# Float64 weight words turned into float32 with a leaky rectifier, and a new planned order, in an attention and gated-MLP kernel

## The chip, the cores and the metric

The kernel runs on one core of one Trainium2 chip. The metric is the device time of one execution in microseconds. A core has a matrix engine (TensorE, PE in the profile), three engines for elementwise work (VectorE or DVE, ScalarE or ACT, GpSimd or POOL), and SyncE (SP), which here issues all transfers between the main memory and the on-chip memory SBUF. TensorE writes its sums to the memory PSUM.

## The reference

There are 8 batches of 576 positions. In each, 8 heads of width 64 compute masked softmax attention; heads 0 to 3 see the last 32 positions, heads 4 to 7 see earlier positions that are congruent modulo 32. The heads' outputs, side by side, are the input x (576 by 512) of a gated MLP:

```
scores = where(mask, (q @ k.T) / 8, -1e9);  attn = exp(scores - max) / (sum + 1e-9)
x      = attn @ v                               # all heads, (B, 576, 512)
h      = maximum(x @ w_in, 0);  u, v = halves of h, 512 columns each
v_n    = (v - mean(v)) / sqrt(var(v) + 1e-6)    # over the 512 columns
v_s    = w_spatial @ v_n + b_spatial[:, None]   # over the positions
out    = (u * v_s) @ w_out
```

q, k, v and w_spatial come as float32. w_in (512 by 1024) and w_out (512 by 512) come as float64. The diff is about how these two reach the chip's arithmetic.

## The kernel before

**Work and tiles.** Two heads make an attention tile t; four tiles make a batch, the first two of them local (heads 0 to 3), the other two strided. A tile is loaded as q, k and v, its scores are formed on TensorE (`s`), masked, exponentiated and normalised on the three elementwise engines, turned by a VectorE transpose (`pc`), copied piece by piece into the layout of the next matmul (`ptl` for local tiles, `pts` for strided), multiplied by v on TensorE (`po`), and written as x.

**Three products for one.** Each float32 operand of the large products is split into a high part, rounded to TensorE's format (`rnd`, a one-input copy), and a low part, the rest (`rest`, a two-input subtraction, L372). Every product is then three matmuls: high by high, high by low, low by high. This holds for x, w_in, w_spatial, the normalised v (`vn`), the gated values (`g`) and w_out.

**Stages of a batch.** `moe_1` forms the v half of h (L800), its statistics (L767 to L780), the normalisation (L787) and the split, and the u half (L842). `moe_tail` does the last 64 positions. `moe_2` applies w_spatial (L922, L934, L935), multiplies by u (L944) and projects (L964). The two weights must be on the chip in split form before a batch's products with them can run, and w_spatial with its tail rows `wtail` before `moe_2`.

**Float64 weights.** `weight` loads a 128 by 512 piece of w_in or w_out (a "half" of w_in is such a piece of its u or its v columns) as pairs of 32-bit words and turns it into float32 in place. There are twelve pieces. Read as a float32, the top word has the sign, eight of the eleven exponent bits, and then three exponent bits and twenty mantissa bits where a float32 has its mantissa. The steps are: multiply the top word, as a float32, by 2**-112, which moves the exponent to float32's bias (L674 on ScalarE or L676 on VectorE); shift the low word right by 29 (L681); shift the top word left by 3 and merge it with the low bits (L688), which pushes the sign out; merge the sign back in (L696). `rnd` and `rest` then split the result into `w_in_sb` or `w_out_sb`.

**Staging space.** The first four pieces use the later space of `vn`; the following pieces alternate between the two buffers each of `u` and `g`. The raw spatial weights and wtail use buffers of the x ring, which has eight. q, k and v have two buffers each, so a load of a third tile waits until the first one's is used.

**Order.** Nothing is written in order by hand. Every step is added to a `Program` with a key (its due time), the engines that could do it and a cost on each. `order` then plays the program forward: each engine takes the ready step with the lowest key, and a step that several engines could do goes to the one that ends it first. KEYS holds the due times: `a` of the first eight attention tiles, `v` and `u` of the pieces of w_in by block of rows, `o` those of w_out, `s` and `t` of w_spatial and wtail, `fill` and `cst` of the setup. A weight's load is due 25 before its key, a tile's q, k and v 34, 33 and 20 before. Later steps have due times by their place in the plan of batches. `near` is how far ahead in keys TensorE looks for another attention matmul once it is in that mode. Before the time `dpt` (in thousands of ns) the planner adds the charge `dp` to VectorE's end time wherever it compares VectorE with another engine for a step:

```python
            held = KEYS["dp"][0] if now < KEYS["dpt"][0] * 1000.0 else 0.0
            other = [
                (begin(n, o, max(free[o] + queue(o, n), ready_at[n][o])) + c + held * (o == DVE), o)
                for o, c in ops[n][1]
                if o != e
            ]
            if other and min(other)[0] < now + cost + held * (e == DVE):
                e = min(other)[1]
```

A step's `port` names engines on which the planner holds it back while the other of VectorE and GpSimd runs a step that has itself such a mark. `rnd` steps have the mark (DVE,), `rest` steps that may run on GpSimd (DVE, POOL); the normalisation of the scores (L416) and the subtraction of the row maximum (L570) also have (DVE, POOL). Before WARM_END, `fillers` adds matmuls on zeros (L1085) into TensorE's long planned gaps.

Of the kernel before, what the change touches and what calls it, by code (L numbers as in the profile page):

```python
# [12 lines left out]
AF = mybir.ActivationFunctionType  # L13
ALU = mybir.AluOpType
# [22 lines left out]
TAIL = S - 4 * P  # L37
NT = 4
KEYS = {
    "a": (-2171.5, -625.6, -893.2, -356.9, 1325.6, -222.2, -52.3, 22.3,),  # L40
    "v": (-407.2, -245.7, -878.2, -1404.4,),
    "u": (-86.3, -477.1, 14.3, -106.1,),
    "s": (434.1, 1240.4, 3115.7, 449.8,),
    "o": (212.8, 23.8, 371.3, 2176.0,),
    "t": (1572.7,),
    "lead": (0.24,),
    "dp": (2136,),
    "dpt": (102.36,),
    "fill": (-432.8, 2205.8, 217.3, 421.5, 2743.1, 2393.8,),
    "cst": (-952.3,),  # L50
    "near": (280.07,),
}
WARM_END, WARM_GAP, WARM_COST, WARM_COLS, WARM_SHARE = 110000.0, 800.0, 427.0, 256, 0.5
FETCHED, FETCH_COST = 200.0, 32.0
# [5 lines left out]
PE, ACT, DVE, POOL, DMA = "tensor", "scalar", "vector", "gpsimd", "sync"  # L60
# [67 lines left out]
class Program:  # L128
# [37 lines left out]
    def order(self):  # L166
# [37 lines left out]
        while len(issued) < len(ops):  # L204
            best = None
            for e in ENGINES:
                while wait[e] and taken[wait[e][0][1]]:
                    heapq.heappop(wait[e])
                while ready[e] and taken[ready[e][0][1]]:
                    heapq.heappop(ready[e])  # L210
                if ready[e]:
                    at = free[e]
                elif wait[e]:
                    at = max(free[e], wait[e][0][0])
                else:
                    continue
                if best is None or at < best[0]:
                    best = (at, e)
            now, e = best
            while wait[e] and wait[e][0][0] <= now:  # L220
                n = heapq.heappop(wait[e])[1]
                if not taken[n]:
                    heapq.heappush(ready[e], (ops[n][0], n))
            n = heapq.heappop(ready[e])[1]
            if e == PE:
                stock = min(FETCHED, stock + (now - since) / FETCH_COST)
                since = now
                other = []
                if n in self.tiled:
                    if self.tiled[n] > stock:  # L230
                        other = [op for op in ready[PE] if op[1] not in self.tiled]
                elif mode:
                    other = [
                        op for op in ready[PE]
                        if self.tiled.get(op[1], FETCHED) < stock
                        and op[0] < ops[n][0] + KEYS["near"][0]
                    ]
                if other:
                    heapq.heappush(ready[PE], (ops[n][0], n))
                    ready[PE].remove(min(other))  # L240
                    heapq.heapify(ready[PE])
                    n = min(other)[1]
            cost = dict(ops[n][1])[e]
            if e == PE:
                cost += 45.0 * ((n in self.tiled) != mode)
                mode = n in self.tiled
                stock -= self.tiled.get(n, 3)
                cost += FETCH_COST * max(0.0, -stock)
            now = begin(n, e, max(free[e], ready_at[n][e]))
            held = KEYS["dp"][0] if now < KEYS["dpt"][0] * 1000.0 else 0.0  # L250
            other = [
                (begin(n, o, max(free[o] + queue(o, n), ready_at[n][o])) + c + held * (o == DVE), o)
                for o, c in ops[n][1]
# [4 lines that stand above are left out]
                cost = dict(ops[n][1])[e]  # L258
                now = begin(n, e, max(free[e], ready_at[n][e]))
            taken[n] = True  # L260
            if e in self.port.get(n, ()):
                held_by[e] = (now, now + cost)
            free[e] = now + cost
            issued.append((now, n, e))
            for m in after[n]:
                for o in ENGINES:
                    lag = LAT[e][o]
                    ready_at[m][o] = max(ready_at[m][o], now + cost + lag)
                left[m] -= 1
                if not left[m]:  # L270
                    release(m)
# [34 lines left out]
def attention_moe(ctx, tc, qT, kT, vl, vs, cst, w_in, w_out, wsp, wtail, out):  # L306
# [6 lines left out]
    add = prog.add  # L313
# [341 lines left out]
    def weight(key, src, n, dst, tok, stage):  # L655

        buf, i = stage
        if src.dtype == F32:  # L660
            val = lambda: buf().bitcast(F32).rearrange(FLAT[len(buf.ring.shape)])[:, 2 * i * n : 2 * i * n + n]
            load(key - 25, val, src, [(buf, i, 0), (buf, i, 1)], P * n * 4)
        else:
            raw = lambda dt: buf().bitcast(dt).rearrange(FLAT[len(buf.ring.shape)])[
                :, 2 * i * n : 2 * (i + 1) * n
            ]
            half = lambda j, dt=I32: raw(dt).rearrange("p (n t) -> p n t", t=2)[:, :, j]
            low, top = (buf, i, 0), (buf, i, 1)
            val = lambda dt=F32: half(1, dt)
            load(key - 25, lambda: raw(I32), src.bitcast(I32), [low, top], P * n * 8)  # L670

            def scale(eng):
                if hasattr(eng, "activation"):
                    eng.activation(val(), val(), AF.Copy, scale=2.0**-112)  # L674
                else:
                    eng.tensor_scalar(val(), val(), 2.0**-112, None, op0=ALU.mult)  # L676

            add(key, [(ACT, 95 + 0.833 * n), (DVE, 70 + 0.52 * n)], scale, [], [top], port=(DVE, POOL))
            add(
                key, [(DVE, 70 + 0.52 * n)],  # L680
                lambda eng: eng.tensor_scalar(  # L681
                    half(0), half(0), 29, None, op0=ALU.logical_shift_right
                ),
                [], [low], port=(DVE, POOL),
            )
            add(
                key, [(DVE, 70 + 1.04 * n)],
                lambda eng: eng.scalar_tensor_tensor(  # L688
                    half(0), half(1), 3, half(0),
                    op0=ALU.logical_shift_left, op1=ALU.bitwise_or,  # L690
                ),
                [top], [low], port=(DVE, POOL),
            )
            add(
                key, [(DVE, 70 + 1.04 * n)],
                lambda eng: eng.scalar_tensor_tensor(  # L696
                    half(1), half(1), -0x80000000, half(0),
                    op0=ALU.bitwise_and, op1=ALU.bitwise_or,
                ),
                [low], [top], port=(DVE, POOL),  # L700
            )
        lo_in = [(buf, i, 0), (buf, i, 1)] if src.dtype == F32 else [top]
        rnd(key, n, lambda: dst(0), val, lo_in, [(*tok, 0)])
# [290 lines left out]
    lead = min(nb, 2)  # L994
# [168 lines left out]
```

## Time and profile before

| | |
|---|---|
| median of 3 runs | 540.17 us (539.29 to 542.32) |
| profiled execution | 543.93 us, its span 542.1 us |
| mean granted TensorE clock | 0.984 of full speed |
| PE busy | 515.1 us (95%), 6500 matmuls |
| DVE busy | 323.9 us (60%) |
| ACT busy | 235.5 us (43%) |
| POOL busy | 127.7 us (24%) |
| transfers | 52.65 MB, 97 GB/s over the span |

Busy shares are means over the whole span. The page's slices, 13.55 us each, show how they are spread; the chain of waits follows the work that ended last back in time; the listings by line give a group's count, its busy time and the mean of one.

### The profile page before, as it was taken

What the parts mean: (1) busy time and instruction counts of PE and PEld (TensorE: products, weight loads), DVE (VectorE), ACT (ScalarE), POOL (GpSimd) and SP (SyncE); (2) the same over time, 40 slices, a digit from 0 to 9 for tenths busy, and PEclk for the clock granted to TensorE, in tenths of its full rate; (3) what the DMA queues carried; (4) which work ended last, traced back from release to release, by engine and by line L of the source; (5) the groups of instructions that cost most, each with busy time, mean ns of one, the idle gap of its engine ahead of it and who ended that gap; (6) DMA issues with size and microseconds to landing.
All of it is one profiled execution on the core that took longest, in us unless ns stands there. A gap on an engine that the chain in (4) does not pass through costs nothing.

```text
span 542.1 us, 15698 instructions
## 1 busy us (share of the span) xinstructions
PE 515.1 (95%) x6500; PEld 471.4 (87%) x6500; DVE 323.9 (60%) x1026; ACT 235.5 (43%) x751; POOL 127.7 (24%) x215
## 2 busy tenths in 40 slices
PE   3779889999999999999899999999999999999997
PEld 1547869989899899998899888998989989998997
DVE  3797988267684678737573486943774271435232
ACT  5676769455551564514531464422641232212211
POOL 2877778431220132003010031100310020001000
PEclk8889989999999999999989999999999999999999
DMA  8787845152251325312141424211121200110011
GB/s 234 269 239 220 287 131 156 38 173 86 77 180 45 108 77 159 129 45 77 33 125 47 130 75 137 84 46 44 54 70 45 83 1 1 34 44 13 1 45 44
DMA packets 26102, 52.65 MB, mean 97 GB/s; under 512 B 3120, under 2 KB 11440, under 8 KB 26032
## 3 DMA queue, kind: packets, MB, share of 16 engines
q1 hardware_dynamic: 26032, 51.65, 30.6%
q8 instruction: 51, 0.84, 0.7%
q14 instruction: 19, 0.16, 0.1%
HBM read 42.21 MB, written 9.44 MB: 95 GB/s over the span
## 4 chain that ended last, share of the span: by engine, by line
PE 83%; DVE 6%; DMA 4%; POOL 2%; issue 2%; SPq 1%; ACT 0%; POOLq 0%; ACTq 0%; DVEq 0%
PE m L964 19%; PE m L922 18%; PE m L800 17%; PE m L842 17%; PE po L609 3%; PE po L514 3%; DMA g<-w_in 2%; PE s L432 2%; PE m L934 2%; DMA kbd<-kT 2%; PE m L935 2%; PE s L542 2%; SPq L391 1%; POOL ptl L364 1%; DVE vv L787 1%
## 5 line engine op out<-in xcount | busy, mean ns | idle before, releaser
L922 PE MATMUL m<-wsp_sb,vn 128*128 128x288 f32 x768 | 111.0, 295 | 0.3 <-issue 0.3
L842 PE MATMUL m<-x,w_in_sb 128*128 128x288 f32 x768 | 107.8, 299 | 2.4 <-ACT vv L762 1.3
L842 PEld LDWEIGHTS m<-x,w_in_sb 128*128 128x128 f32 x768 | 104.7, 190 | 4.5 <-ACT vv L762 1.5
L922 PEld LDWEIGHTS m<-wsp_sb,vn 128*128 128x128 f32 x768 | 105.5, 189 | 1.2 <-issue 0.5
L964 PE MATMUL m<-g,w_out_sb 128*128 128x288 f32 x768 | 106.2, 297 | 0.0
L964 PEld LDWEIGHTS m<-g,w_out_sb 128*128 128x128 f32 x768 | 103.4, 188 | 0.6
L800 PE MATMUL m<-w_in_sb,x 128*128 128x512 f32 (+1 forms) x408 | 100.9, 403 | 2.2 <-ACT u L856 2.2
L800 PEld LDWEIGHTS m<-w_in_sb,x 128*128 128x128 f32 (+1 forms) x408 | 74.8, 187 | 21.8 <-ACT u L856 2.4
L384 ACT COPY o<-m 128x288 f32<-128x288 f32 x61 | 24.1, 397 | 118.1 <-PE m L964 110.2
L780 POOL TENSOR_TENSOR bn<-bn,sel 128x1 f32<-128x1 f32 (+1 forms) x37 | 21.4, 577 | 226.0 <-DVE bn L775 221.9
L944 DVE TENSOR_TENSOR u<-m,u 128x288 f32<-128x288 f32 x64 | 28.2, 453 | 61.7 <-PE m L935 61.6
L469 ACT ACTIVATE pl<-pl,ml 128x64 f32<-128x64 f32 (+1 forms) x160 | 53.6, 339 | 1.8 <-DVE ml L452 1.4
L767 DVE BATCH_NORM_STATS2 bn<-vv 128x6 f32<-128x512 f32 (+1 forms) x37 | 25.4, 687 | 42.0 <-ACT vv L762 41.9
L364 POOL TENSOR_SCALAR ptl<-pc 32x64 f32<-32x64 f32 (+3 forms) x83 | 32.9, 396 | 68.7 <-PE po L514 52.7
L856 ACT ACTIVATE u<-m 128x288 f32<-128x288 f32 x64 | 25.8, 409 | 36.8 <-PE m L842 35.5
L762 ACT ACTIVATE vv<-m 128x512 f32<-128x512 f32 (+1 forms) x37 | 22.0, 596 | 44.8 <-PE m L800 43.9
L372 DVE TENSOR_TENSOR x<-po,x 128x288 fp32r<-128x288 f32 x64 | 27.0, 448 | 20.3 <-ACT x L384 19.9
L787 DVE TENSOR_SCALAR vv<-vv,bn 128x512 f32<-128x512 f32 (+1 forms) x37 | 23.3, 630 | 13.1 <-POOL bn L780 13.0
L469 ACT ACTIVATION_READ_ACCUMULATOR pl<-pl,ml 128x1 f32 (+1 forms) x160 | 30.5, 191 | 0.0
L362 ACT COPY ptl<-pc 32x64 f32<-32x64 f32 (+3 forms) x77 | 26.1, 339 | 6.9 <-DVE pc L485 3.9
L384 ACT CAST x<-po 128x288 fp32r<-128x288 f32 x49 | 18.5, 397 | 17.3 <-PE po L609 9.1
L372 DVE TENSOR_TENSOR g<-u,g 128x288 fp32r<-128x288 f32 x56 | 25.2, 460 | 1.1
(113 smaller groups left out, 599.3 us busy)
## 6 DMA issues: line engine op xcount, KB each, us to landing
q<-qT SPq DMA_DIRECT2D x32, 295.0 KB, 4.7
outT<-o SPq DMA_DIRECT2D x64, 144.0 KB, 1.8
v_raw<-vs SPq DMA_DIRECT2D x16, 512.0 KB, 4.4
v_raw<-vl SPq DMA_DIRECT2D x16, 384.0 KB, 3.7
k<-kT SPq DMA_DIRECT2D x16, 304.0 KB, 4.8
kbd<-kT SPq DMA_DIRECT2D x32, 144.0 KB, 5.4
vn<-w_in SPq DMA_DIRECT2D x4, 512.0 KB, 8.6
x<-wsp SPq DMA_DIRECT2D x4, 288.0 KB, 5.7
```

What stands on the lines that cost most here:

```text
L362: eng.copy(dst(), src())
L364: eng.tensor_scalar(dst(), src(), 1.0, 0.0, op0=ALU.mult, op1=ALU.add)
L372: eng.tensor_tensor(dst(), src(), f32(hi()), op=ALU.subtract)
L384: eng.copy(dst(), src())
L469: eng.activation(p_sb()[:m, u, :], p_sb()[:m, u, :], AF.Exp, bias=st()[:m, u : u + 1], scale=-1.0, accum_out=st()[:m, NU + u : NU + u + 1],)
L787: lambda eng: eng.tensor_scalar(v()[:m], v()[:m], bn()[:m, 6:7], bn()[:m, 9:10], op0=ALU.subtract, op1=ALU.mult),
L800: eng.matmul(v_ps()[:m, :], x_at(kt)[:, a, :], w_in_sb[:, w, kt, HF:], start=(kt == 0 and i == 0), stop=(kt == NT - 1 and i == 2),)
L842: eng.matmul(u_ps()[:, :HS], w_in_sb[:, w, kt, f * P : (f + 1) * P], xs[NHP * b + kt]()[:, a, r], start=(kt == 0 and i == 0), stop=(kt == ...
L856: lambda eng, u=u, f=f, u_ps=u_ps: eng.activation(u()[:, f * HS : (f + 1) * HS], u_ps()[:, :HS], AF.Relu),
L922: eng.matmul(s_ps()[:, :HS], vn()[:, a, kt, fs], wsp_sb[:, w, kt, r], start=(kt == 0 and i == 0), stop=False,)
L944: lambda eng, ug=ug, s_ps=s_ps: eng.tensor_tensor(ug(), s_ps()[:, :HS], ug(), op=ALU.mult),
L964: eng.matmul(o_ps()[:, :HS], w_out_sb[:, w, f, e * P : (e + 1) * P], g[a]()[:, f, :], start=(f == 0 and i == 0), stop=(f == NT - 1 and i = ...
```

## The change

It does four things. The scale of the top word becomes a leaky rectifier (`AF.Prelu`) on ScalarE alone: it computes the word times 2**-112 where that is positive, and 2**32 times this where it is negative. The added 32 in the exponent field of a negative number is the bit that the following left shift by 3 moves into the sign's place, so the shift-and-merge gives the signed float32, which now goes to the top half, and the last merge is gone. The marks of the remaining conversion steps change from (DVE, POOL) to (DVE,). `dp` gets two values: the first for steps without POOL in their mark (one-input copies above all), the second, negative, for steps with it (two-input work); `dpt` goes from 102.36 to 111.4. And all due times in KEYS are new.

```diff
 KEYS = {
-    "a": (-2171.5, -625.6, -893.2, -356.9, 1325.6, -222.2, -52.3, 22.3,),
-    "v": (-407.2, -245.7, -878.2, -1404.4,),
-    "u": (-86.3, -477.1, 14.3, -106.1,),
-    "s": (434.1, 1240.4, 3115.7, 449.8,),
-    "o": (212.8, 23.8, 371.3, 2176.0,),
-    "t": (1572.7,),
-    "lead": (0.24,),
-    "dp": (2136,),
-    "dpt": (102.36,),
-    "fill": (-432.8, 2205.8, 217.3, 421.5, 2743.1, 2393.8,),
-    "cst": (-952.3,),
-    "near": (280.07,),
+    "a": (-386.4, -359.7, -266.9, -216.9, 87.6, 27.0, 41.5, 68.7,),
+    "v": (-371.9, -323.9, -273.0, -212.6,),
+    "u": (2.8, -132.8, -60.4, -51.2,),
+    "s": (38.6, 78.9, 221.1, -22.2,),
+    "t": (373.9,),
+    "o": (37.3, 7.7, 245.9, 18,),
+    "cst": (-524.5,),
+    "lead": (-0.6,),
+    "fill": (-179.6, -350.1, -489.2, 258.8, -409.1, -194.5,),
+    "dp": (2179, -1565,),
+    "dpt": (111.4,),
+    "near": (83.1,),
 }
...
-            held = KEYS["dp"][0] if now < KEYS["dpt"][0] * 1000.0 else 0.0
+            locks = POOL in self.port.get(n, ())
+            held = KEYS["dp"][locks] if now < KEYS["dpt"][0] * 1000.0 else 0.0
...
-            def scale(eng):
-                if hasattr(eng, "activation"):
-                    eng.activation(val(), val(), AF.Copy, scale=2.0**-112)
-                else:
-                    eng.tensor_scalar(val(), val(), 2.0**-112, None, op0=ALU.mult)
-
-            add(key, [(ACT, 95 + 0.833 * n), (DVE, 70 + 0.52 * n)], scale, [], [top], port=(DVE, POOL))
+            add(
+                key, [(ACT, 95 + 0.833 * n)],
+                lambda eng: eng.activation(val(), val(), AF.Prelu, scale=2.0**-112, alpha=2.0**32),
+                [], [top],
+            )
             add(
                 key, [(DVE, 70 + 0.52 * n)],
                 lambda eng: eng.tensor_scalar(
                     half(0), half(0), 29, None, op0=ALU.logical_shift_right
                 ),
-                [], [low], port=(DVE, POOL),
+                [], [low], port=(DVE,),
             )
             add(
                 key, [(DVE, 70 + 1.04 * n)],
                 lambda eng: eng.scalar_tensor_tensor(
-                    half(0), half(1), 3, half(0),
+                    half(1), half(1), 3, half(0),
                     op0=ALU.logical_shift_left, op1=ALU.bitwise_or,
                 ),
-                [top], [low], port=(DVE, POOL),
-            )
-            add(
-                key, [(DVE, 70 + 1.04 * n)],
-                lambda eng: eng.scalar_tensor_tensor(
-                    half(1), half(1), -0x80000000, half(0),
-                    op0=ALU.bitwise_and, op1=ALU.bitwise_or,
-                ),
-                [low], [top], port=(DVE, POOL),
+                [low], [top], port=(DVE,),
             )
```

## Rows read from the trace of the kernel before

**Rows 1.** The page's slices of the span, 40 of 13.55 us each.

```profile
PE   3779889999999999999899999999999999999997
DMA  8787845152251325312141424211121200110011
```

**Rows 2.** Early stretches: length, busy time and count of each engine, clock, DMA share, GB/s.

```profile
0.00:13.00 13.00, 4.83 (x80) 2.33 (x80) 4.37 (x28) 6.62 (x20) 3.35 (x14) 0.86 0.81 226
13.00:27.20 14.20, 10.86 (x307) 7.25 (x308) 10.98 (x41) 9.88 (x38) 11.29 (x16) 0.86 0.80 273
27.20:44.00 16.80, 12.62 (x253) 8.12 (x253) 14.87 (x46) 11.54 (x43) 12.04 (x14) 0.92 0.87 237
44.00:53.50 9.50, 9.50 (x116) 7.37 (x116) 7.87 (x18) 6.66 (x16) 7.17 (x10) 1.00 0.80 234
53.50:72.60 19.10, 16.39 (x244) 15.21 (x239) 19.08 (x32) 12.13 (x24) 15.81 (x15) 1.00 0.71 248
...
74.00:111.00 37.00, 36.99 (x473) 33.91 (x471) 20.43 (x95) 25.20 (x99) 21.05 (x30) 0.95 0.31 97
```

**Rows 3.** TensorE by line to 74 us, the fillers: busy us, mean ns, idle before.

```profile
L1085 PE MATMUL s<-zeros 128*32 128x256 f32 x38 | 13.2, 508 | 1.0 <-DVE zeros L1044 0.9
```

**Rows 4.** The chain that ended last, in order of time: start us, us, what.

```profile
32.06 11.78 DMA g<-w_in
...
53.47 0.68 DVE u L688
...
71.90 0.67 DVE wsp_sb L372
...
73.74 4.56 PE m L800 x12
```

**Rows 5.** VectorE by line and shape from 53.5 to 72.6 us.

```profile
L787 DVE TENSOR_SCALAR vv<-vv,bn 128x512 f32<-128x512 f32 x4 | 4.5, 1124 | 0.8 <-POOL bn L780 0.8
L696 DVE SCALAR_TENSOR_TENSOR u<-u 128x512 int32<-128x512 int32 x2 | 2.6, 1303 | 0.0
L407 DVE TENSOR_SCALAR mx<-mx 128x16 f32<-128x16 f32 x2 | 2.2, 1084 | 0.0
L372 DVE TENSOR_TENSOR vn<-vv,vn 128x512 fp32r<-128x512 f32 x1 | 1.4, 1423 | 0.0
...
L372 DVE TENSOR_TENSOR w_out_sb<-u,w_out_sb 128x512 fp32r<-128x512 f32 x1 | 1.2, 1160 | 0.0
...
L696 DVE SCALAR_TENSOR_TENSOR g<-g 128x512 int32<-128x512 int32 x1 | 0.7, 669 | 0.0
```

**Rows 6.** ScalarE's table load, the only one of the whole span.

```profile
L1034 ACT ACT_TABLE_LOAD x1 | 1.3, 1283 | 0.7 <-PEq L1152 0.7
```

**Rows 7.** Line L372 from 53.5 to 72.6 us: VectorE, GpSimd, clock, DMA share, GB/s.

```profile
53.50:72.60 19.10, 4.22 (x5) 11.67 (x8) 1.00 0.71 248
```

**Rows 8.** Single lines over the span: durations min/median/max in ns, first and last start.

```profile
L787 DVE TENSOR_SCALAR vv<-vv,bn x37: 494/547/1529, 52.7 to 501.3; 128x512 f32<-128x512 f32 x35, 64x512 f32<-64x512 f32 x2
L407 DVE TENSOR_SCALAR mx<-mx x16: 158/175/1266, 19.5 to 407.4; 128x16 f32<-128x16 f32 x16
L372 DVE TENSOR_TENSOR vn<-vv,vn x29: 635/684/1423, 69.3 to 502.3; 128x512 fp32r<-128x512 f32 x29
L416 DVE TENSOR_TENSOR pp<-p,mx x12: 458/459/460, 115.8 to 408.2; 128x288 f32<-128x288 f32 x12
L416 DVE TENSOR_TENSOR pl<-pl,ml x10: 817/824/827, 131.8 to 389.6; 128x640 f32<-128x640 f32 x10
L416 POOL TENSOR_TENSOR pl<-pl,ml x6: 1261/1350/1522, 16.2 to 97.0; 128x640 f32<-128x640 f32 x6
```

**Rows 9.** Line L364, GpSimd's copies into `ptl`: durations min/median/max in ns.

```profile
L364 POOL TENSOR_SCALAR ptl<-pc x83: 236/381/852, 18.6 to 399.5; 32x64 f32<-32x64 f32 x27, 32x320 f32<-32x320 f32 x22, 32x128 f32<-32x128 f32 x19, 32x256 f32<-32x256 f32 x15
```

**Rows 10.** Transfers from 0 to 74 us.

```profile
DMA packets 6901, 18.11 MB, mean 245 GB/s; under 512 B 846, under 2 KB 974, under 8 KB 6890
```

## The prediction

> **What bounds the kernel now.** I read the slices of the page first. The PE row begins with 3, 7 and 7 and is at 9 from the seventh slice almost to the end, while the DMA row is at 7 to 8 through the first five slices and then falls to 5 and less [rows 1]. So the time splits in two: an opening of some 74 us in which TensorE waits, and a rest in which it hardly does. The early stretches say how much is lost: in the first three TensorE is busy for 4.83 + 10.86 + 12.62 = 28.3 of 44.0 us, then for 9.50 of 9.5 and for 16.39 of 19.1, and from 74 to 111 us for 36.99 of 37.0 [rows 2]. Part of the early busy time is not work: 38 filler matmuls on zeros take 13.2 us before 74 us [rows 3]. Whatever this change brings must be found in the opening, because after it every microsecond is a matmul that the diff leaves as it is.
>
> The chain of waits says what holds the opening. It passes one wait of 11.78 us for the transfer of a w_in half, from 32.06 to 43.84 us; from 53.47 us it goes along VectorE, one instruction after the other, until the low half of a spatial weight at 71.90 + 0.67 = 72.57 us; then TensorE starts at 73.74 us [rows 4]. In that last stretch VectorE is busy for 19.08 of 19.1 us, GpSimd for 15.81, ScalarE for 12.13, and the DMA share is 0.71 [rows 2]. So two things are tight there, VectorE wholly and the DMA engines nearly, and TensorE's own idle time is only 19.1 - 16.39 = 2.7 us.
>
> **The change part by part.**
>
> *The merge that goes.* Each of the twelve converted pieces of w_in and w_out loses one 512-wide two-input instruction on VectorE (L696). Three of the twelve lie in the last stretch: 2.6 us for two and 0.67 for one, 3.3 us in all; one of them is far over the others' 0.67, because something held it [rows 5]. The other nine lie where the chain runs through transfers, GpSimd or TensorE; I cost them at nothing, covered by the 11.78 us transfer wait before all else.
>
> *The rectifier in place of the scale.* It is one ScalarE instruction per piece where there was one. Most of the twelve were on ScalarE already; those that the planner gave to VectorE must now go there too. No row shows the new function. Below, I bound it at no change, since it is one pass over the same 512 columns with immediates. Above, it could need another function table beside Exp: the trace has one table load, of 1283 ns, in the whole execution, though Exp, Relu and plain copies alternate [rows 6]. Two loads for each of twelve pieces would be 24 x 1.283 = 30.8 us of ScalarE. I take no change, the nearest row being that one load for three functions. The Trainium skill (ScalarE: Activation LUTs, Table sets: the hidden batching unit) says that cheap functions sit in every set and a switch costs a load and a drain, but its list of fillers does not name the leaky rectifier; by its 2.7 us a switch, an estimate, 24 switches would be 64 us instead of 30.8.
>
> *Two-input work towards VectorE.* The planner so far charged VectorE 2136 ns for any piece that another engine could also do, before 102 us. Now one-input pieces are charged 2179 and two-input ones are given 1565 in VectorE's favour, before 111 us. In the last stretch GpSimd runs eight L372 subtractions for 11.67 us [rows 7], and a normalisation and a max subtraction of 288 columns. If all ten go to VectorE they cost eight times 0.684 us (the 512-wide median there; two of the eight are 576 wide, a little more) and two times 0.459: 6.4 us [rows 8].
>
> What VectorE gets back is the time in which it stood behind GpSimd. Against their medians the four L787 (the first begins just ahead of the stretch) took 4.5 - 4 x 0.547 = 2.3 us too long, the two L407 2.2 - 2 x 0.175 = 1.8, and the two L372 1.42 + 1.16 - 2 x 0.684 = 1.2: together 5.3 us [rows 5, 8]. A 16-column instruction that takes 1.08 us instead of 0.175 does not compute longer, it waits. If GpSimd has only copies left, whose median is 0.381 us against 1.35 for a 640-wide normalisation [rows 8, 9], most of it goes. The balance of the stretch is 3.3 + 5.3 - 6.4 = 2.2 us shorter. The bounds: if nothing moves but the merges go, 3.3 shorter; if all moves and no wait goes, 6.4 - 3.3 = 3.1 longer. I take 2.2, which TensorE's 2.7 us of idle in that stretch can give back.
>
> Against this speaks a rule of the Trainium skill (SBUF — State Buffer, Who interferes with whom): a VectorE instruction with two SBUF inputs and a GpSimd instruction that reads SBUF share one port pair, and the one that starts first holds it to its end. By it the moved subtractions would block GpSimd's copies and be blocked by them. The trace bears the rule out on the side of GpSimd's copies too: a ptl copy takes up to 0.852 us against a median of 0.381 [rows 9]. It makes the first rival below.
>
> *The same move earlier.* The normalisation of local scores takes GpSimd 1.350 us and VectorE 0.824 [rows 8]. Three stand in the first 74 us and two of them on the chain; 2 x 0.526 = 1.1 us. If VectorE's queue is full there the gain is 0, or a loss as large as their 0.824 each. In 13 to 27 us VectorE is at 10.98 of 14.2 [rows 2], so there is room; I keep 1.1.
>
> *The new order.* The due times are written anew, so every piece's loads move in SyncE's queue, with the conversions and attention steps behind them. Sorted, the first loads now are tile 0, v-half 0, tile 1, v-half 1, tile 2, v-half 2, tile 3, v-half 3, then the four u-halves with one row block of the spatial weights among them, and only then w_out, the second batch's tiles and the other spatial rows. Before, u-half 1 stood ahead of tile 3, and tile 5 of the second batch ahead of the last u-halves. From the shapes a local tile loads 1.007 MB, a strided one 1.121, a half 0.524; so all of the first batch with w_in is through after 4.26 + 4.19 + 0.10 + 0.29 = 8.84 MB. At the rates read, 226 x 13.0 + 273 x 14.2 = 6.82 MB are in by 27.2 us and the rest at 237 GB/s by 35.7 us [rows 2], 8 us ahead of the 43.8 us at which the chain's transfer ended. This is the upper bound, since the two-deep rings for q, k and v can hold the queue as they do now. The lower bound is 0: the sum of bytes stays, 18.11 MB had to come before 74 us at 245 GB/s [rows 10], and the tail and last spatial rows, which are due latest (373.9 and 221.1), close the opening. TensorE's idle between 27.2 and 44 us is 16.80 - 12.62 = 4.2 us [rows 2]; I take under half of it, 1.8, as the DMA share there is 0.87.
>
> *After 111 us* the planner's tie window for attention matmuls shrinks from 280 to 83 and attention is due 0.84 later. TensorE covers this at 36.99 of 37.0 us; I cost it at nothing and allow 1 us either way.
>
> **Sum.** 2.2 + 1.1 + 1.8 = 5.1 us less. The profiled execution took 543.93 us (span 542.1 and 1.83 around it), so its like would take 538.8. It stands 3.76 us over the median of the runs, 540.17, and above all three; its difference should carry over: 535.1 us.
>
> **The rivals.**
>
> *VectorE becomes fuller than it was.* Place: 53 to 73 us. The ten moved pieces cost 6.4 us, the three merges return 3.3, and the waits stay because GpSimd's copies and VectorE's subtractions hold one another: 3.1 us longer, 543.3 us. It decides from the point at which less than 3.1 of the 5.3 us of waits goes. For it: VectorE has 0.02 us free in the stretch. Against it: the held instructions there are the ones beside 1.3 to 1.8 us subtractions. 0.17.
>
> *The transfers hide it.* The opening lasts until 18.11 MB are in, whoever computes; VectorE's gain turns into waits for wtail and the last spatial rows. For it: 0.71 to 0.87 DMA share. This is also the outcome if the planner hardly moves anything. 540 us, 538 to 542. 0.26.
>
> *The order is worth its bound.* The first batch's products start 8 us earlier and stay ahead; with 2.2 + 1.1 and 7 us for the order the time is about 530. For it: the 11.78 us on the chain. Against: TensorE is nearly full from 44 us on, and what it would do next needs the later loads. 0.14.
>
> *Table loads.* If the rectifier is in another set than Exp, ScalarE gets up to 30.8 us more before 80 us; up to 72.6 us it is busy for 46.8 us [rows 2] and has room for some 25 of it, but not when it is needed. Half of it late gives 555 us. 0.03.
>
> **How the numbers follow.** My forecast, 533 to 537.4 us, has 0.40. About 0.5%, 2.7 us, is what a measurement of this kernel can tell from no change. Faster is forecast and order, 0.54, and a little of the transfers case: 0.56. Same is most of that case with the weak end of the first rival: 0.26. Slower is the rest, 0.18. The range runs from 528.5 (order at its bound and all terms good) to 543.5 (the first rival at full price).
>
> **What would show it.** L696 gone and one ACT_TABLE_LOAD; ScalarE's twelve rectifiers near the old length. GpSimd with few L372, L416 and L570 before 111 us, and L407 and L787 on VectorE near 0.175 and 0.547. The last w_in half landing before 40 us. TensorE without gaps from about 69 us instead of 73.7. If VectorE is solid to 73 us again or GpSimd's copies double, the first rival is right; if TensorE's last early wait is for wtail or wsp, the second. The prediction is wrong if the time saved lies after 111 us, or if TensorE's steady stretch starts no earlier.

## The result, and the profile after

The changed kernel takes 534.09 us (median, 533.77 to 535.09), the kernel before, measured beside it, 539.73 us (539.15 to 542.32): a ratio of 0.9889 [0.9854, 0.9925], 5.6 us or 1.1% faster. Its profiled execution took 534.34 us, with a span of 532.5 us at a mean granted clock of 0.984. The slices answer to [rows 1]:

```profile
PE   7798999999999999999899999999999999999997
DMA  8879643542243223312321325211121200110011
```

TensorE starts at 7 instead of 3 and is at 9 from the fifth slice on (but for one 8 later), instead of from the seventh. The same early stretches as in [rows 2]:

```profile
0.00:13.00 13.00, 9.35 (x165) 4.58 (x166) 5.02 (x33) 8.82 (x28) 3.92 (x15) 0.87 0.85 281
13.00:27.20 14.20, 11.14 (x188) 7.75 (x187) 11.05 (x42) 11.41 (x41) 5.04 (x11) 0.76 0.88 265
27.20:44.00 16.80, 15.67 (x271) 12.58 (x267) 16.62 (x40) 11.26 (x24) 5.96 (x9) 1.00 0.77 242
44.00:53.50 9.50, 7.49 (x45) 7.25 (x44) 8.05 (x35) 7.47 (x28) 4.17 (x4) 0.82 1.02 278
53.50:72.60 19.10, 18.62 (x269) 16.40 (x268) 17.31 (x38) 12.96 (x33) 5.94 (x10) 1.00 0.56 183
...
74.00:111.00 37.00, 36.67 (x609) 33.26 (x603) 24.07 (x110) 24.98 (x101) 9.83 (x26) 1.00 0.54 162
```

Up to 44 us TensorE is busy for 36.2 us instead of 28.3, and with fewer fillers: those take 6.7 + 3.4 = 10.1 us up to 74 us instead of 13.8. VectorE, solid from 53.5 to 72.6 us before, is now solid from 27.2 to 44 us (16.62 of 16.8), while GpSimd has fallen to six tenths or less from 13 us on. The chain of waits, against [rows 4] (start, duration, what):

```profile
35.00 0.60 DVE g L688
...
37.27 6.14 DMA g<-w_out
...
45.75 0.61 DVE vn L373
46.45 0.61 ACT vv L754
47.10 11.38 PE m L834 x72
...
63.11 4.44 DMA x<-wtail
```

The wait for a w_in half is gone. Behind the first load of k, the transfers on the chain are now one of w_out and wtail. The load of w_out goes into a buffer `g` that VectorE's conversions leave at 37.27 us; from its landing the chain goes through the next conversions, VectorE's vn subtraction and ScalarE's copy of the v block out of PSUM (L754), for which TensorE waits. TensorE's timeline (start, duration, line, waits in brackets) shows where its solid work begins:

```profile
41.62 3.46 PE L834 MATMUL m<-x,w_in_sb 128*128 128x288 f32 x24
...
47.10 11.38 PE L834 MATMUL m<-x,w_in_sb 128*128 128x288 f32 x72 [2.01 <-ACT vv L754]
...
71.35 0.37 PE L927 MATMUL m<-wt_b,tail_b 97*128 97x288 f32 x1 [0.48 <-DVE wt_b L744]
...
103.81 10.77 PE L792 MATMUL m<-w_in_sb,x 128*128 128x512 f32 x45
```

The steady start, after which no wait up to 111 us is longer than 0.48 us, is at 47.10 us instead of 73.74 [rows 4]; wtail, although on the chain, costs TensorE only 0.48 us. The last row is the second batch's v block. In a second profile of the kernel before (run before_again, below) its like is found at 111.25, in the first at 113.20 us.

The rows by line and shape, 0 to 111 us (count, busy us, mean ns, idle before). ScalarE:

```profile
L676 ACT ACTIVATE vn<-vn 128x512 f32<-128x512 f32 x4 | 2.7, 681 | 0.0
L676 ACT ACTIVATE g<-g 128x512 f32<-128x512 f32 x4 | 2.7, 672 | 3.0 <-DMA g<-w_out 3.0
L1026 ACT ACT_TABLE_LOAD x1 | 1.3, 1283 | 0.7 <-PEq L1144 0.7
```

The rectifier takes 0.67 to 0.68 us per piece and brings no second table load [rows 6]. VectorE:

```profile
L779 DVE TENSOR_SCALAR vv<-vv,bn 128x512 f32<-128x512 f32 x5 | 2.9, 581 | 0.2
L408 DVE TENSOR_SCALAR mx<-mx 128x16 f32<-128x16 f32 x5 | 1.0, 197 | 0.1
L373 DVE TENSOR_TENSOR vn<-vv,vn 128x512 fp32r<-128x512 f32 x4 | 2.7, 684 | 0.5 <-POOL vn L365 0.5
L681 DVE TENSOR_SCALAR u<-u 128x512 int32<-128x512 int32 x4 | 1.6, 400 | 0.0
```

The first three are L787, L407 and L372 of before: 581 ns where [rows 5] had 1124 from 53.5 to 72.6 us, 197 where it had 1084 (over the same 0 to 111 us, four of L407 had a mean of 772 ns), 684 where it had 1423 for the one of four that was not on GpSimd. GpSimd:

```profile
L772 POOL TENSOR_TENSOR bn<-bn,sel 128x1 f32<-128x1 f32 x5 | 3.4, 701 | 6.8 <-DVE bn L763 5.2 <-DVE bn L767 1.5
L365 POOL TENSOR_SCALAR vn<-vv 128x512 fp32r<-128x512 f32 x1 | 2.4, 2414 | 0.4 <-ACT vn L363 0.4
```

The one-column L772 is now GpSimd's only two-input work before 111 us. Over the span GpSimd is busy for 82.2 us instead of 127.7.

### The profile page after: what moved, and what is told of

Its sections match the earlier page's. It is cut to its first block, busy times and chain, and to the rows that moved or that the text cites. A ratio compares the mean times of both kernels' runs of the same rounds, so it can differ in the third digit from the quotient of the medians.

```text
span 532.5 us, 15665 instructions
## 1 busy us (share of the span) xinstructions
PE 514.2 (97%) x6490; PEld 471.8 (89%) x6490; DVE 324.3 (61%) x1060; ACT 235.9 (44%) x745; POOL 82.2 (15%) x175
## 4 chain that ended last, share of the span: by engine, by line
PE 82%; DVE 9%; DMA 3%; ACT 2%; issue 2%; SPq 1%; POOL 0%; DVEq 0%; ACTq 0%
PE m L956 19%; PE m L834 19%; PE m L792 16%; PE m L914 15%; PE po L610 3%; PE po L515 3%; PE s L433 2%; PE s L543 2%; PE m L926 2%; PE m L927 2%; ACT pl L470 1%; DMA g<-w_out 1%; DVE x L373 1%; DMA x<-wtail 1%; SPq L392 1%
## 5 line engine op out<-in xcount | busy, mean ns | idle before, releaser
L385 ACT COPY o<-m 128x288 f32<-128x288 f32 x58 | 22.9, 398 | 114.6 <-PE m L956 106.6
L772 POOL TENSOR_TENSOR bn<-bn,sel 128x1 f32<-128x1 f32 (+1 forms) x37 | 22.0, 596 | 222.9 <-DVE bn L767 216.8
L365 POOL TENSOR_SCALAR ptl<-pc 32x320 f32<-32x320 f32 (+3 forms) x83 | 32.6, 393 | 109.0 <-PE po L515 65.2
L759 DVE BATCH_NORM_STATS2 bn<-vv 128x6 f32<-128x512 f32 (+1 forms) x37 | 25.3, 686 | 36.3 <-ACT vv L754 36.2
L754 ACT ACTIVATE vv<-m 128x512 f32<-128x512 f32 (+1 forms) x37 | 22.1, 598 | 45.8 <-PE m L792 45.0
L373 DVE TENSOR_TENSOR x<-po,x 128x288 fp32r<-128x288 f32 x64 | 27.4, 449 | 23.2 <-ACT x L385 23.0
L453 DVE CUSTOM_DVE_ANT_0 pl<-s,cst_sb 128x64 f32<-128x64 f32 (+1 forms) x160 | 25.7, 216 | 8.1 <-PE s L433 8.0
L373 DVE TENSOR_TENSOR g<-u,g 128x288 fp32r<-128x288 f32 x62 | 27.8, 454 | 2.0 <-ACT g L363 0.5
L779 DVE TENSOR_SCALAR vv<-vv,bn 128x512 f32<-128x512 f32 (+1 forms) x37 | 20.5, 554 | 13.9 <-POOL bn L772 13.5
```

Source lines behind the costliest of these rows:

```text
L365: eng.tensor_scalar(dst(), src(), 1.0, 0.0, op0=ALU.mult, op1=ALU.add)
L373: eng.tensor_tensor(dst(), src(), f32(hi()), op=ALU.subtract)
L385: eng.copy(dst(), src())
L453: eng.tensor_tensor_reduce(out=p_sb()[:m, u, :], in0=s_ps[u % 2]()[:m, f0 : f0 + 2 * STRIDE], in1=msk[:m], scale=-SCALE, scalar=3.0e38, op ...
L759: lambda eng: eng.bn_stats(bn()[:m, 0:6], v()[:m]), [(v,)], [(bn,)],
```

## The experiments

The theories. A: VectorE is the bound of the opening, and the change shortens its work, by the merge and by the waits behind GpSimd that go. B: the order of the loads is the gain, the rest is hidden. C: the due times, the split of work and the weight path are fitted to one another, and none carries a gain alone. Beside A in the last pair stands F: what counts is GpSimd's own lateness, not what it does to VectorE.

**Each part alone.** The change has three parts that can be switched one by one: the weight path (rectifier, one merge), the split (`dp`, `dpt`) and the due times. The new marks of the conversion steps are not switched by themselves: they go with the weight path in w_alone and with the split in split_alone. A part that is off has the text of before; the planner then makes its own order.

```diff
# w_alone: after's weight path; KEYS of before, dp (2136, 2136), dpt 102.36
# split_alone: before's weight path and due times
+    "dp": (2179, -1565,), "dpt": (111.4,),
# and its conversion steps marked port=(DVE,)
# times_alone: before's weight path, dp and dpt
+    "a" ... "fill", "near": as after
```

> The weight path alone: leaky rectifier and one merge less, with the due times, the single charge of 2136 ns for VectorE and the limit of 102.36 us of before; the planner places everything anew from that. Theory A (VectorE's load is the gain): three merges of the last opening stretch go, 3.3 us, and nothing comes to VectorE in their place, about 537 us. Theory B (the order of loads and attention is the gain): 539 to 540 us, the freed time turns into waits for transfers. Theory C (due times, split and weight path are fitted to one another, and a part alone is worth nothing): 539 to 543 us.

> The split charge alone (2179 ns against one-input work on VectorE, 1565 ns for two-input work, up to 111.4 us), with the four conversion steps and the due times of before; the conversion's steps are marked as one-input work so that the scale stays off VectorE as before. Theory A: in the last stretch 5.3 us of waits go and 6.4 us of work come, so 1 us longer at 541 us, and GpSimd's two-input lines are nearly empty before 111 us. Theory B: 540 us. Theory C: 542 us or more.

> The new due times alone, with the old weight path and the single charge of before. Theory A: little, 538 to 540 us, since VectorE has its old load and still stands behind GpSimd. Theory B: most of the gain, 534 to 536 us, with the u products of the first batch starting before 45 us instead of at 53.9. Theory C: 541 us or more.

Measured: the weight path alone 538.5 us, 0.9978 [0.9958, 0.9997]; the split alone 544.64, 1.0084 [1.0057, 1.0111]; the due times alone 542.28, 1.0047 [1.0027, 1.0067]. The split alone is slower than before, and VectorE fuller: 84.5 us of work up to 111 us against 78.6 and 81.8 in the two profiles of before, and again solid from 53.5 to 72.6 us, where TensorE has 14.57 us of work (16.39 in [rows 2]):

```profile
53.50:72.60 19.10, 14.57 (x263) 12.02 (x262) 19.08 (x42) 10.85 (x24) 4.88 (x6) 0.93 0.78 278
```

Of the waits of TensorE up to 111 us (who for whom: us, times, longest) the greatest is one that the kernel before has too. The split alone:

```profile
PE s L543 <- DMA kbd<-kT: 7.2, 1, 7.2
```

The kernel before:

```profile
PE s L542 <- DMA kbd<-kT: 9.3, 2, 7.0
```

The due times alone lack this wait and have others:

```profile
PE po L515 <- POOL ptl L365: 6.4, 4, 2.1
PE po L610 <- POOL pts L365: 3.5, 3, 2.1
```

and its stretch from 27.2 to 44 us:

```profile
27.20:44.00 16.80, 12.24 (x212) 9.22 (x212) 15.56 (x28) 10.65 (x25) 12.73 (x14) 0.90 0.70 249
```

With the old due times TensorE waits some 7 us for a transfer of k, whatever VectorE gains. That is no loss against before, but it shows what the split cannot reach. With the new due times and the old split the attention waits for copies that stand behind two-input work on GpSimd, which is busy for 12.73 us of the stretch. So B falls: the order alone makes the kernel slower. The three add up to +1.1%, the whole is -1.1%: the parts are not a sum, as C says. C's words for the weight path are too strong: alone it gains 0.2%, with an interval that just excludes no change, while A's 537 us is not reached either.

**The changed kernel with one part undone.** no_split and old_times undo one part and let the planner order anew; old_path does so with the weight path.

```diff
# no_split
-    "dp": (2179, -1565,), "dpt": (111.4,),
+    "dp": (2136, 2136), "dpt": (102.36,),
# old_times: "a" ... "fill", "near" of before; path and split of after
# old_path: before's scale and two merges, marked port=(DVE,); due times and split of after
```

> The changed kernel without the split of the charge (both 2136 ns, limit 102.36 us), planned anew from the new due times. Theory A (VectorE's work and its waits behind GpSimd set the opening): GpSimd runs two-input work again, VectorE stands behind it for some 5 us, and what it loses in work it gets back only in part: 537 to 539 us. Rival D (the split moves load but gains nothing): 533 to 535 us, as the changed kernel. Theory C (only the three together): 539 us or more.

> The changed kernel with the due times of before (weight path and split new), planned anew. Theory A: 535 to 537 us, since VectorE has the same work. Theory B (order of loads): 539 to 541 us, with TensorE's wait for the kbd transfer back at 7 us or more. Theory C: 540 us or more.

> The changed kernel with the weight path of before (plain scale and two merges, marked as one-input work), the split and the new due times kept, planned anew. Theory A: 538 to 540 us, as merge_back, since VectorE has the 8.2 us again in an opening that it bounds. Theory C: 541 us or more. If planning anew can step round the merges: 536 us or less.

Measured: no_split 538.66, 0.9971 [0.9948, 0.9995]; old_times 536.98, 0.9935 [0.9906, 0.9965]; old_path 542.41, 1.0023 [0.9994, 1.0053]. Against the changed kernel's 0.9889 they give back 0.8, 0.5 and 1.3% (each times 540 us: 4.4, 2.5 and 7.2 us), 14 us where the whole is worth 5.6. The changed kernel was not measured again beside these runs, so each difference has the width of two intervals, some 0.4 to 0.5% either way: clear for no_split and old_path, at the edge for old_times. Each part is worth more when the other two are there. In its strict form, that only the three together gain, C falls: without the new due times the other two still gain 0.65% (old_times, in A's range; no_split is in A's range too, old_path in C's). In no_split the stretch from 27.2 to 44 us reads:

```profile
27.20:44.00 16.80, 13.31 (x118) 9.39 (x118) 15.02 (x26) 10.83 (x23) 14.96 (x16) 0.80 0.64 221
```

GpSimd is at 14.96 instead of 5.96 and TensorE at 13.31 instead of 15.67. In old_times TensorE waits for the transfer of k again, as before:

```profile
PE s L543 <- DMA kbd<-kT: 7.9, 2, 6.8
```

**The merge put back, order kept.** The replanned kernels change the order too. merge_back keeps the changed kernel's order exactly and gives every piece a second merge as long as the one removed.

```diff
-                lambda eng: eng.scalar_tensor_tensor(
-                    half(1), half(1), 3, half(0), ...),
+                lambda eng: (
+                    eng.scalar_tensor_tensor(half(0), half(1), 3, half(0),
+                        op0=ALU.logical_shift_left, op1=ALU.bitwise_or),
+                    eng.scalar_tensor_tensor(half(1), half(1), 0, half(0),
+                        op0=ALU.bitwise_and, op1=ALU.bitwise_or),
+                ),
```

> The changed kernel with its order of instructions kept exactly, and the second merge put back behind the first in each of the twelve pieces (the first one writes the low half, the second moves it to the top half with a mask of zero, so the value is the same): 12 x 0.68 = 8.2 us more on VectorE. Theory A: what the merges were worth comes back, 3.3 us or more on the path, 537 to 539 us. Theory B: VectorE has room in the new order, at most 1 us, 535 us. Theory C says nothing of it, since the order is kept.

Measured: 539.53 us, 0.9987 [0.9967, 1.0006]. Twelve merges of 0.7 to 0.8 us on average, 5.3 us lost against the changed kernel (0.98%, some 0.4% either way), nearly the whole gain. TensorE's timeline and the window:

```profile
51.95 11.35 PE L840 MATMUL m<-x,w_in_sb 128*128 128x288 f32 x72 [2.27 <-ACT vv L760]
```

```profile
27.20:44.00 16.80, 14.41 (x190) 11.04 (x189) 16.46 (x35) 10.45 (x22) 4.21 (x8) 0.90 0.60 202
```

The steady start moves from 47.10 to 51.95 us. VectorE is as solid from 27.2 to 44 us as in the changed kernel (16.46) and simply gets through less. Most of the merges lie on the path: in this order nothing covers them. Of the twelve, eight stand on the chain that ended last before 51.95 us, 5.8 us together. Three of them (start, duration, what):

```profile
42.04 0.69 DVE u L693
...
43.90 0.70 DVE g L693
...
48.40 0.69 DVE u L693
```

**One more VectorE instruction less.** no_low_bits leaves out the low word, so that the last three mantissa bits of w_in and w_out are zero; order and placing stay.

```diff
-                lambda eng: eng.tensor_scalar(
-                    half(0), half(0), 29, None, op0=ALU.logical_shift_right
-                ),
+                lambda eng: None,
...
-                lambda eng: eng.scalar_tensor_tensor(half(1), half(1), 3, half(0), ...),
+                lambda eng: eng.tensor_scalar(
+                    half(1), half(1), 3, None, op0=ALU.logical_shift_left),
```

> The changed kernel with its order kept exactly and less conversion work on VectorE: the low word is left out (no shift of it, and the top word is only shifted left by 3), so the last three mantissa bits of w_in and w_out are zero. Per piece 0.42 us of shift goes and the 0.68 us merge becomes a one-input shift of about 0.42: 0.68 us less, 8.2 us over twelve, as much as the merge that merge_back put back. Theory A: VectorE is still the bound from 10 to 47 us, and the time falls by about what merge_back cost, 5 us, to 529 us. Rival E: VectorE's bound is used up and transfers or ScalarE come next, 532 to 534 us.

Measured: 529.78 us (527.45 to 533.95), 0.9821 [0.9768, 0.9874].

```profile
45.12 9.86 PE L831 MATMUL m<-x,w_in_sb 128*128 128x288 f32 x72 [0.28 <-ACT vv L751]
```

```profile
27.20:44.00 16.80, 15.10 (x255) 12.31 (x256) 13.82 (x35) 12.33 (x26) 3.78 (x8) 1.00 0.81 258
```

VectorE is no longer solid (13.82), the start comes 2.0 us earlier, and TensorE's wait there for ScalarE's copy (L751, L754 in the changed kernel) is 0.28 instead of 2.01 us. The direction is A's. It is faster than the kernel before by 1.8%; against the changed kernel the two intervals just overlap (0.7%, some 0.6% either way), and the price is those bits. Not all of that difference, 4.3 us between the medians, need be VectorE's: this execution was granted 1.00, the level of 2.4 GHz, in every stretch of the opening, the changed kernel 0.76 to 0.87 in three of them, a mean of that level and 1.2 GHz.

**The two-input work back on GpSimd, order kept.** two_input_pool issues on GpSimd those two-input steps that were planned on VectorE before 111.4 us and may run on either.

```diff
-        for _, n, e in issued:
+        for at, n, e in issued:
+            if e == DVE and at < 111400.0 and POOL in self.port.get(n, ()) \
+                    and POOL in dict(self.ops[n][1]):
+                e = POOL
```

> The changed kernel with its order kept exactly, but every two-input step that may run on either engine and begins before 111.4 us by the plan is issued on GpSimd: 46 of them, which cost VectorE about 46 x 0.6 = 28 us and GpSimd some 50. If only the load of VectorE counted, the opening would get shorter by several us, to 530. Theory A with waits: each is slower on GpSimd (1.35 instead of 0.82 us, 1.4 instead of 0.68) and stands in the chain of its tile or weight, and VectorE's one-input work waits behind it: 542 to 552 us, with GpSimd busy over 14 of 16.8 us from 27 to 44 us.

Measured: 544.69 us, 1.0093 [1.0069, 1.0117]. Against the changed kernel 2.0% (some 0.4% either way), 11.0 us, are lost, more than the whole gain.

```profile
27.20:44.00 16.80, 14.01 (x182) 10.96 (x179) 11.12 (x21) 10.02 (x21) 13.66 (x15) 0.80 0.50 164
```

```profile
PE po L517 <- POOL ptl L367: 4.6, 4, 1.9
PE m L928 <- POOL tail L375: 3.1, 1, 3.1
```

VectorE falls to 11.12 us of work and GpSimd rises to 13.66; TensorE now waits for GpSimd's copies and for its slow subtractions. The granted clock up to 111 us was 0.89 on the mean where the changed kernel had 0.94, so a part of the loss may be the clock's. This order belongs to this split.

**Do GpSimd's reads hold VectorE?** idle_subtract puts two 256-column subtractions of zeros on GpSimd beside each two-input step of VectorE before 111 us (76 in all); idle_memset, meant as control, five 256-column memsets instead, which read nothing. The order stays.

```diff
+            if e == DVE and 5000.0 < at < 111400.0 and POOL in self.port.get(n, ()) ...:
+                for _ in range(2): nc.gpsimd.tensor_tensor(scratch, zero, zero, op=ALU.subtract)
# idle_memset instead:
+                for _ in range(5): nc.gpsimd.memset(scratch, 0.0)
```

> The changed kernel with its order kept, and beside each of VectorE's two-input steps that may run on either engine (those between 5 and 111.4 us of the plan, some 45) two subtractions of 256 columns on GpSimd whose result nobody reads: about 1.2 us of two-input work on GpSimd each, VectorE's own work unchanged. Theory A (VectorE and GpSimd hold one another while both read SBUF): VectorE's shifts, normalisations and merges get longer, its busy time before 111 us rises by 8 us or more at an unchanged count, and the time goes to 541 us or more. Rival F (GpSimd's extra work only delays GpSimd's own copies): the same time as idle_memset, within 1 us.

> The control of idle_subtract: in the same places GpSimd writes zeros with five memsets of 256 columns, about as much of its time (1.2 to 1.4 us), but reading nothing. Theory A: VectorE's durations stay as in the changed kernel, its busy time before 111 us within 2 us of 83.5; only GpSimd's copies come later, 535 to 538 us, several us under idle_subtract. Rival F: as idle_subtract.

Measured: 553.84 us, 1.0248 [1.0227, 1.0268], and 559.35 us, 1.0345 [1.0321, 1.0369]. The control missed its expectation widely. idle_subtract, GpSimd and VectorE:

```profile
L302 POOL TENSOR_TENSOR scratch<-zeros 128x256 f32<-128x256 f32 x76 | 56.0, 737 | 5.5
...
L380 DVE TENSOR_TENSOR vn<-vv,vn 128x512 fp32r<-128x512 f32 x4 | 3.9, 990 | 0.5 <-POOL vn L372 0.5
```

and TensorE's waits:

```profile
PE po L522 <- POOL ptl L372: 10.0, 4, 6.4
```

The same views of idle_memset:

```profile
L301 POOL MEMSET scratch<- 128x256 f32 x185 | 59.5, 322 | 10.3
...
L377 DVE TENSOR_TENSOR vn<-vv,vn 128x512 fp32r<-128x512 f32 x4 | 2.7, 685 | 0.5 <-POOL vn L369 0.5
...
L685 DVE TENSOR_SCALAR u<-u 128x512 int32<-128x512 int32 x4 | 2.0, 511 | 0.0
```

```profile
PE po L519 <- POOL ptl L369: 14.7, 4, 9.5
```

The durations answer the question, the times do not. The vn subtraction takes 990 ns beside reading GpSimd work, 685 beside memsets and 684 in the changed kernel. Summed over VectorE's groups up to 111 us (count times the difference of the group's mean from the changed kernel's), VectorE is held for 9.6 us in idle_subtract, 1.1 in idle_memset, 0.9 in merge_back, 7.3 in two_input_pool, 11.0 in no_split, and 12.8 and 14.2 in the two profiles of before. The same sum is 12.5 us in w_alone, which gains, and 1.0 in split_alone, which loses: freeing VectorE of these waits does not by itself make the kernel faster. By the Trainium skill (SBUF — State Buffer, Who interferes with whom) a VectorE instruction with two SBUF inputs contends with a GpSimd instruction that reads SBUF and not with one that only writes it; the 990 against 685 ns agree. But the memsets took up GpSimd for longer than the subtractions (59.5 against 56.0 us), and TensorE waited longer for its copies (14.7 against 10.0 us, 1.4 in the changed kernel). The difference of those waits, 4.7 us, is near the 5.5 us between the two times. For the times of this pair F's mechanism is the likelier one, though its expectation, the same time within 1 us, failed too; and the pair cannot price VectorE's waits. A's expected rise of VectorE's busy time did not come either (79.6 us up to 111 us), since fewer of its instructions ran by then, 244 instead of 297.

**The kernel before, a second time.** before_again is the unchanged kernel before, to see what two profiles of one program differ by.

> The kernel before once more, unchanged, for a second profile: its first one stood 3.8 us over the median. If that excess is a chance of one execution, this one's span is nearer to 538 us, and the stretches from 10 to 30 and from 70 to 80 us, whose granted clock was 0.69 to 0.83, show where it lay. If not, the span is 542 us again.

Measured: 539.59 us, 1.0003 [0.9978, 1.0027]. Its timeline:

```profile
71.54 3.00 PE L800 MATMUL m<-w_in_sb,x 128*64 128x512 f32 x12 [2.21 <-ACT u L856]
...
111.25 10.66 PE L800 MATMUL m<-w_in_sb,x 128*128 128x512 f32 x45
```

Its span is 536.7 us where the first one's was 542.1. The opening (to the second batch's v block) ends 2.0 us earlier, and what follows is 3.4 us shorter: 536.7 - 111.25 = 425.4 against 542.1 - 113.20 = 428.9. Most of the excess thus lay behind the early stretches in which it was looked for. The tail block is the same twelve matmuls in both: 3.00 us here, 4.56 in [rows 4]. A difference of some 3 us between two single profiles is thus no evidence here.

## Why the prediction was right, and which of its steps were wrong

**The time and the place.** Forecast 535.1 us, 533 to 537.4 as its own range; measured 534.09. The saving lies in the opening, as said: the second batch's v block comes 113.20 - 103.81 = 9.4 us earlier (7.4 against before_again), and what follows it takes 428.7 us in the changed kernel, 428.9 and 425.4 before. The profiled execution of before was 4.2 us over its median, the one of after 0.25 over its own, so the 9.6 us between the two spans come to 9.6 - 4.2 + 0.25 = 5.65 us between the medians. Against before_again 3 us of the opening's gain would be given back behind 104 us; whether the new order costs something there or the clock did, no run settles. The cause, as far as the runs show it: the gain is a joint one. With the new order VectorE's conversions are on the path (merge_back), and this order needs the new split (two_input_pool, no_split); how much of the split's share is VectorE's waits, how much GpSimd's lateness and how much the clock stays open.

**The merge: the mechanism right, nine of twelve mis-sized.** I took 3.3 us for the three merges in the last stretch and nothing for the other nine, "covered by the 11.78 us transfer wait". That step failed. The new order removes this very wait, so what it covered comes into the open. Put back in the unchanged order the twelve cost 5.3 us (merge_back), and not in the stretch I named: from 53.5 to 72.6 us TensorE is as busy there with the second merge (19.10 us) as without it (18.62). Eight of them are paid before 52 us. With the old order and the old split, where the prediction's own bound for the merges alone was 3.3 us, they bring 1.2 us (w_alone).

**Two-input work towards VectorE: the direction right, size and place off.** Terms 5.3 - 6.4 + 1.1 make the move worth nothing on balance. With the new order it is worth 11.0 us (two_input_pool, order kept) or 4.4 (no_split, replanned); alone it costs 4.5 (split_alone, 0.84% of 540 us). The waits behind GpSimd that I read in one stretch (5.3 us) add up to 12.8 to 14.2 us over the whole opening. And I priced the move by VectorE's queue alone; a part of it is GpSimd's: free of 1.3 to 1.8 us subtractions, it has the attention copies ready in time. How the two share it is not shown. One reading for it was weak: the spread of the ptl copies, 0.381 to 0.852 us [rows 9], mixes four widths, whose means up to 111 us run from 251 to 580 ns, so it does not by itself show that VectorE held them. The observation named for it held: L408 and L779 near their short durations, no L373, L417 or L571 on GpSimd before 111 us. I took their going out of the stretch from 53.5 to 72.6 us as the gain; there TensorE did get 2.2 us back (18.62 against 16.39), but 7.9 us came before 44 us (3.1 and 5.2 against before_again). TensorE's steady start, forecast for about 69 us, came at 47.10.

**The order of loads: what it does right, what it is worth not a term.** The last w_in half's low part is written by VectorE at 40.51 + 0.69 = 41.2 us, and the shift of its low word begins at 38.13, so it was on the chip before 40 us as forecast. I gave this 1.8 us. By itself it costs 2.5 us (times_alone, 0.47%), undone it costs 2.5 (old_times, at the edge of the noise). What the due times do is seen in both: TensorE's wait of some 7 us for k is gone in times_alone and back in old_times. Early data help TensorE only where VectorE and GpSimd keep up with them: 12.24 us busy from 27.2 to 44 us in times_alone, as the 12.62 before, 15.67 with all three parts. A sum of three terms has no place for that; that it came out at 5.1 for a measured 5.6 is partly the luck of errors that cancel: merges too cheap, moves too cheap, both shares of one joint gain.

**The rectifier** at no change: right, one table load. **After 111 us** nothing: right against the first profile, open within 3 us by the second.

**The rivals.** *VectorE becomes fuller*: it does, 83.5 us of work up to 111 us against 78.6 and 81.8 in the two profiles of before, but earlier, when the loads are in. With the split alone the rival's outcome came true: solid to 72.6 us and 544.6 us, for its 543.3. There VectorE's waits had gone (1.0 us left), so the moved work filled it, not the holding. The holding of copies by subtractions shows in the changed kernel on GpSimd's wide copies: 2.41 us for the 128x512 copy into vn, 0.85 and 0.98 us for two into w_in_sb, where before five took 0.66 to 0.74; none of them is on the chain. *The transfers hide it*: they are the next bound in part (6.14 us for w_out on the chain, a DMA share of 1.02 from 44 to 53.5 us, where TensorE loses 2.0 us), but they do not eat the gain. The sign named for this rival did appear, in small: TensorE's wait at 71.35 us, 0.48 us, is for wtail's low part. *The order is worth its bound*: fell, alone it is a loss, and the whole is 534 us, not 530. *Table loads*: fell.

## What to carry to other kernels

A cost is hidden only as long as its cover stays: when a change also removes the wait that covered an instruction, price that instruction again as if in the open. Where a planner's due times, its split between engines and a step's length change together, run each alone and each undone; here the three were worth -1.2, +4.5 and +2.5 us alone and -5.6 together, and a sum of terms can be right by accident. An instruction that takes several times its own median is a wait, and the sum over all groups of count times that excess shows how much an engine is held by its neighbour. It does not price the time: here a run with 1.0 us of it was slower than one with 12.5.

## What was not expected of the hardware

GpSimd's 256-column memset took 322 ns and its two-input subtraction of the same width 737. Memsets left VectorE's two-input subtractions as they were (685 ns) while its one-input shift of 512 columns had a mean of 511 instead of 400 ns. That is not so each time: amid rows of memsets it took 0.59 us twice (at 31.89 and 44.54 us) and 0.42 once (49.72), and no run says what decides. The granted clock of a stretch differs between executions without a row that says why: from 13 to 27.2 us it was 0.76 (a mean of 2.4 and 1.2 GHz) in the changed kernel, where TensorE ran 188 matmuls in 11.14 us, and 1.00 in no_low_bits, where it ran 198 in 9.30; and the kernel before had 0.95 from 74 to 111 us in one profile, after the idle time that ends at 73.74 [rows 2, 4], and 1.00 in the other, whose tail block starts after a wait of 2.21 us too.
